# A planner that keeps the shared SBUF port of VectorE and GpSimd as a resource: decay attention and an expert layer on one core

## The chip, the core and the metric

The kernel runs on one core of a Trainium2 chip. TensorE (PE) multiplies matrices, VectorE (DVE), ScalarE (ACT) and GpSimd (POOL) work on elements, and SP issues most DMAs. The metric is the device time of one execution in microseconds; for several runs it is the median. The changed kernel will be compared with this one on the same chip.

## The reference

Attention with a decay per position (8 batches, 8 heads, 576 positions, 64 per head), and its output is the input of an expert layer (4608 tokens, 512 to 2048 to 512):

```python
scores = scale * np.matmul(q, k.transpose(0, 1, 3, 2))
log_f = np.log(np.clip(f, 0.0001, 1.0))
cum = np.cumsum(log_f, axis=-1)
decay = cum[:, :, :, None] - cum[:, :, None, :]
scores = np.where(causal, -1000000000.0, scores + decay)
scores = scores - np.max(scores, axis=-1, keepdims=True)
attn = np.exp(scores)
attn = attn / (np.sum(attn, axis=-1, keepdims=True) + 1e-09)
attn_out = np.matmul(attn, v)
...
h = x @ w_in
g = np.where(pos, h, np.where(neg, 0.0, (h + beta) ** 2 / (4.0 * beta)))
return g @ w_out
```

## The kernel before

**Two stages, run into each other.** Attention runs in 36 jobs: a job is a batch, a pair of heads and a range of row blocks of 128 positions (the first batch is cut in two ranges, so eight jobs). For each row block GpSimd makes the decay term (L965) and masks it (L969), TensorE makes the scores (L798 or L877), VectorE adds the two and takes the extreme of each row (L1002), ScalarE takes the exponential and its sum (L1011), a small addition on `nm` (L1017, on GpSimd or VectorE) and a reciprocal (L1023, VectorE) make the factor of each row. In the first eight jobs a diagonal matrix with these factors is made (`pr <- ident, nm`, on GpSimd, VectorE or ScalarE), TensorE transposes with it in float32 (L1052, L1058), and multiplies with v (L917). In later jobs the probabilities are split in a high and a low float16 part (L402 or L406, then L1087 on VectorE), a DMA transposes them and TensorE multiplies them (L927).

The expert layer runs in 18 chunks of 256 tokens by 8 blocks of 256 of the inner dimension: TensorE multiplies with w_in (L1150, tile `ph`), ScalarE and VectorE make `u` (L1159, L1162, L1163) and the two float16 parts of `g` (L402, L1169), TensorE multiplies with w_out (L1177, tile `po`).

**Weights.** Each of the 8 blocks of weights has two halves (w_in, w_out). `weight_split` rounds them in place on VectorE (L565, L569, L573, 128x1024 each), ScalarE takes the sum of absolute values (L577), a scale is found through a small transpose on TensorE (`across`, L450 to L465, whose two small steps `top` and `dg` run on VectorE or GpSimd), ScalarE writes the high float16 part (L593), and the low part is made either by VectorE in one instruction (L599) or by GpSimd in two (L601, L602). The raw weights lie in tiles `place` and `x` that are not yet in use, the results in `place`. `moe_scales` makes the scales `z` of the expert layer on GpSimd (L698) and VectorE; `join_scales` (L1121 to L1123) brings two batches to one scale.

**What sets the order.** No order is written out. Every piece of work is given to `Order.op` with its engine, a duration, what it reads and writes, and a priority; some pieces name other engines that may take them (`other`). `Order.plan` then plays through time with these durations: whenever an engine is free, the first piece by priority whose inputs are done and whose buffers can be had is taken, and a piece with several engines goes to the one that is free for it first. The result is one order of emission, and so the order of each engine's queue, the engine of each piece with a choice, and the buffers. On the chip each engine works off its queue in that order and waits only for semaphores; the plan's times play no part there. `OVER`, `AFTER` and the functions `act_us`, `dve_us`, `pool_us` hold the durations. Before, the durations of GpSimd's pieces were longer than they are when it runs alone, and nothing in the plan linked the two engines.

Of the kernel before, what the change touches and what calls it, by code (L numbers as in the profile page):

```python
# [72 lines left out]
class Order:  # L73
    AFTER = {"PE": 0.23, "DVE": 0.04, "ACT": 0.04, "POOL": 0.1, "DMA": 0.06}
    OVER = {"PE": 0.0, "DVE": 0.08, "ACT": 0.093, "POOL": -0.04}
# [9 lines left out]
    def op(self, eng, dur, emit, reads=(), writes=(), prio=0.0, size=0.0, mode=0, other=()):  # L85
        i = len(self.ops)
# [26 lines left out]
        self.ops.append([eng, dur, emit, deps, bufs, prio, size, mode, self.hold])  # L113
        return i

    def plan(self):
# [25 lines left out]
        while done < n:
# [5 lines left out]
            while again:  # L148
                again = False
                for eng, l in waiting.items():  # L150
# [111 lines left out]
def pool_us(n):  # L262
    return 0.3 + 0.00095 * n
# [11 lines left out]
def kernel(  # L275
# [115 lines left out]
    def V(n, emit, reads=(), writes=(), prio=0.0, us=None):  # L391
        op("DVE", us if us else dve_us(n), emit, reads, writes, prio)
# [4 lines left out]
    def G(us, emit, reads=(), writes=(), prio=0.0):  # L397
        op("POOL", us, emit, reads, writes, prio)
# [46 lines left out]
    def across(m, n, mkeys, prio):  # L445
# [17 lines left out]
        op("POOL", 0.7, make, ["ident"], [top, dg], prio, other=[("DVE", 0.4, 0.0)])  # L463
# [21 lines left out]
    def decay_sums():  # L485
# [71 lines left out]
    def weight_split(i, prio):  # L557
        ms = tiny("ms", 2, 2)
        for j in range(2):
# [8 lines left out]
            ), key, [bits], prio, 0.75)  # L568
# [3 lines left out]
            ), key, [bits], prio)  # L572
# [3 lines left out]
            ), [bits], key, prio)  # L576
# [10 lines left out]
        for j in range(2):  # L587
# [16 lines left out]
            op("POOL", 4.35, low, [("sw", i)], key + [("pl", i, j)], prio, other=[("DVE", 1.46, 0.0)])  # L604
# [66 lines left out]
    def moe_scales(b, k, first, last, prio):  # L671
# [38 lines left out]
        G(1.8, make, [("sv", b), ("rv", b), ("lim", k)] + need, [z.key], prio)  # L710
# [5 lines left out]
    def attention(ji):  # L716
# [11 lines left out]
        for j, src in enumerate((q, k)):  # L728
# [73 lines left out]
        else:  # L802
# [58 lines left out]
            V(640, klo, x32[1][2] + [sc, (qs, 1)], [(qs, 2)], pq)  # L861
            V(640, qlo, x32[0][2] + [sc, (qs, 0)], [(qs, 3)], pq)
# [19 lines left out]
        if p >= NPE:  # L882
# [14 lines left out]
            V(640, vlo, vkeys(hp) + [("sv", b), (vs, 0)], [(vs, 1)], pr - 2)  # L897
# [52 lines left out]
        for r in range(r0, r1):  # L950
# [5 lines left out]
            for h in range(2):  # L956
# [17 lines left out]
                G(1.08 + 0.0006 * wid if r < LAST else 1.25, decay, [cks[h], "sdz"] + sigkey, [(sd, h if r == LAST else 0)], pw)  # L974
# [296 lines left out]
```

## Time and profile before

| | us |
|---|---|
| median of 3 runs | 1097.66 (1097.19 to 1098.76) |
| the profiled execution | 1097.19 |
| its span | 1095.4 |
| TensorE busy | 1043.9 |
| VectorE busy | 804.9 |
| ScalarE busy | 729.3 |
| GpSimd busy | 575.2 |

In a row of a timeline stand the start, the length, the engine, the line, the operation, the tiles written and read, their shapes, the count, and in brackets how long the engine had been idle ahead of it and what ended that. In a row of stretches stand the stretch, its length, and for each engine the busy time and the number of instructions, then TensorE's granted clock as a share of full speed, the DMA engines' share and GB/s. In a row of one line's instructions stand the count, then the shortest, the median and the longest duration in ns. In a row of groups stand the count, the busy time in us, the mean in ns, and the idle time ahead of them.

### The profile page before, as it was taken

How to read it: one execution, taken by the hardware profiler on the slowest of the kernel's cores; microseconds unless marked ns; L12 is line 12 of the kernel's file. 1: busy time of each engine (PE TensorE's matmuls, PEld its weight loads, DVE VectorE, ACT ScalarE, POOL GpSimd, SP SyncE). 2: the span in 40 equal slices, each digit the busy share in tenths (PEclk: the TensorE clock that was granted, in tenths of full speed). 3: DMA queues.
4: the chain of work that ended last, by engine and by line, in shares of the span. 5: the costliest groups of instructions: out<-in, count | busy, mean ns of one | idle time of the engine just before them, and what ended most of it. 6: DMA issues, size and time to landing. Idle time of an engine off the chain costs nothing. (4 is left out here: it accounts for less than half of the span.)

```text
span 1095.4 us, 24735 instructions
## 1 busy us (share of the span) xinstructions
PE 1043.9 (95%) x8821; PEld 699.1 (64%) x8821; DVE 804.9 (73%) x2037; ACT 729.3 (67%) x1532; POOL 575.2 (53%) x1023
## 2 busy tenths in 40 slices
PE   6779898999999999999999999999999999999998
PEld 4445555556766666666766666666666777677665
DVE  6889888888778888878888878988887873232232
ACT  4666665767777777777777777777777874344343
POOL 4588866666666665557667656655666740000000
PEclk9889889999999999999999999999999999999999
DMA  7855446668788889778988788888778742000000
GB/s 199 267 153 146 145 105 122 134 107 188 140 176 157 159 163 187 140 153 155 172 167 167 154 166 158 169 168 158 146 147 173 124 105 51 1 20 21 1 20 20
DMA packets 389467, 145.32 MB, mean 133 GB/s; under 512 B 367200, under 2 KB 367200, under 8 KB 389344
## 3 DMA queue, kind: packets, MB, share of 16 engines
q1 hardware_dynamic: 383328, 132.21, 60.9%
q10 hardware_dynamic: 6016, 11.54, 3.0%
q8 instruction: 69, 1.13, 0.4%
q14 instruction: 54, 0.44, 0.1%
HBM read 64.63 MB, written 9.58 MB: 68 GB/s over the span
## 5 line engine op out<-in xcount | busy, mean ns | idle before, releaser
L1150 PE MATMUL ph<-x,place 128*128 128x256 f16 (+3 forms) x4608 | 409.6, 248 | 2.5 <-POOL place L602 1.2
L1177 PE MATMUL po<-place,g 128*128 128x512 f16 x1728 | 403.1, 381 | 1.0 <-ACT g L402 0.8
L1150 PEld LDWEIGHTS <-place 128*128 128x128 f16 x4608 | 357.0, 98 | 54.4 <-issue 5.1
L1177 PEld LDWEIGHTS <-g 128*128 128x128 f16 x1728 | 164.0, 98 | 185.9 <-issue 6.6
L1163 DVE SCALAR_TENSOR_TENSOR u<-ph,z,u 128x512 f32<-128x512 f32 x144 | 107.7, 749 | 127.0 <-ACT u L1162 126.2
L965 POOL TENSOR_SCALAR sdr<-ck,sg,cqs 128x128 f32<-128x128 f32 (+1 forms) x192 | 155.8, 812 | 68.2 <-DVE pr L1087 59.1
L1159 ACT ACTIVATE u<-ph,z 128x512 f32<-128x512 f32 x144 | 110.6, 768 | 103.6 <-PE ph L1150 98.5
L1011 ACT ACTIVATE sdr<-sdr,nm 128x512 f32<-128x512 f32 (+3 forms) x246 | 135.4, 551 | 52.5 <-DVE nm L1002 42.9
L1169 DVE SCALAR_TENSOR_TENSOR g<-u,z,g 128x512 f16<-128x512 f32 x144 | 112.0, 779 | 44.9 <-ACT g L402 44.3
L402 ACT ACTIVATE g<-u,z 128x512 f16<-128x512 f32 x141 | 101.2, 718 | 58.4 <-DVE u L1163 56.6
L1087 DVE SCALAR_TENSOR_TENSOR pr<-sdr,nm,pr 128x128 f16<-128x128 f32 (+1 forms) x224 | 122.3, 575 | 8.6 <-ACT pr L402 5.9
L969 POOL TENSOR_SCALAR_AFFINE_SELECT sdr<-sdr 128x128 f32<-128x128 f32 x246 | 100.6, 409 | 18.1
L1002 DVE CUSTOM_DVE_ANT_0 sdr<-s,sdr,sg 128x128 f32<-128x128 f32 (+1 forms) x192 | 100.6, 541 | 11.6 <-PE s L877 10.0
L402 ACT ACTIVATE pr<-sdr,nm 128x256 f16<-128x256 f32 (+3 forms) x151 | 78.1, 544 | 37.1 <-ACT sdr L1011 11.8
L877 PE MATMUL s<-qkT 128*128 128x128 f16 (+5 forms) x576 | 93.9, 298 | 4.0 <-DVE nm L1002 3.1
L1162 ACT ACTIVATE u<-u 128x512 f32<-128x512 f32 x144 | 90.5, 629 | 4.4
L927 PE MATMUL s<-pT,vs 128*64 128x320 f16 (+4 forms) x1176 | 70.1, 265 | 1.0 <-DVE x L944 0.8
L927 PEld LDWEIGHTS <-vs 128*64 128x64 f16 x1176 | 57.0, 110 | 21.2 <-issue 13.5
L877 PEld LDWEIGHTS <-qkT 128*128 128x128 f16 (+1 forms) x576 | 41.6, 101 | 33.4 <-issue 15.0
L1017 POOL TENSOR_SCALAR nm<-nm 128x2 f32<-128x2 f32 (+1 forms) x68 | 17.5, 257 | 82.7 <-ACT sdr L1011 75.8
L406 POOL TENSOR_SCALAR pr<-sdr,nm 128x512 f16<-128x512 f32 (+3 forms) x73 | 44.2, 608 | 28.5 <-DVE nm L1023 23.0
L965 POOL TENSOR_SCALAR sd<-ck,sg,cqs 64x576 f32<-64x576 f32 x48 | 42.2, 879 | 30.0 <-DVE pr L1087 27.1
(152 smaller groups left out, 1212.8 us busy)
## 6 DMA issues: line engine op xcount, KB each, us to landing
ck<-cum_d SPq DMA_DIRECT2D x62, 288.0 KB, 3.9
out_dram<-ot ACTq DMA_DIRECT2D x36, 256.0 KB, 3.6
v<-in_v_dram SPq DMA_DIRECT2D x64, 128.0 KB, 2.9
qk<-in_k_dram SPq DMA_DIRECT2D x64, 128.0 KB, 2.8
qkT<-qkT SPq DMA_DIRECT2D x48, 160.0 KB, 3.2
qk<-in_q_dram SPq DMA_DIRECT2D x56, 128.0 KB, 3.2
place<-in_moe_w_in_dram SPq DMA_DIRECT2D x8, 512.0 KB, 5.1
x<-in_moe_w_out_dram SPq DMA_DIRECT2D x8, 512.0 KB, 4.1
```

Source lines behind the costliest of these rows:

```text
L402: nc.scalar.activation(out, in_, AF.Copy, scale=scale)
L877: nc.tensor.matmul(sp[p0:p1, 0:c1 - c0], lhsT=tq[:, h, q0 - s0:q0 - s0 + p1 - p0], rhs=tk[:, h, c0:c1], start=(c == 0), stop=(c == 1),)
L927: nc.tensor.matmul(av.ap[64 * h:64 * h + 64, c0:n], lhsT=vs.ap[:, vl, h, t, :], rhs=pT.ap[:, t, pl, h, c0:n], start=(t == 0 and pi == 0), ...
L965: nc.gpsimd.tensor_scalar(out=sd.ap[p0:p1, 0:wid], in0=cks[h].ap[p0:p1, 0:wid], scalar1=ns if p < NQK else ns[p0:p1], scalar2=cqs()[p0:p1, ...
L969: nc.gpsimd.affine_select(sd.ap[p0:p1, q0:wid], sd.ap[p0:p1, q0:wid], pattern=[[-1, wid - q0]], channel_multiplier=1, base=0, compare_op=A ...
L1011: A(wid, lambda i=i, sd=sd, wid=wid, nm=nm, sm=sm: nc.scalar.activation(sd.ap[:, 0:wid], sd.ap[:, 0:wid], AF.Exp, bias=nm.ap[:, i:i + 1], ...
L1087: V(cols, lambda i=i, prv=prv, rows_=rows_, rc=rc: nc.vector.scalar_tensor_tensor(out=prv()[:, :, 1, i, :], in0=rows_(), scalar=rc.ap[:, i ...
L1150: nc.tensor.matmul(ph.ap[:, fi * TC + a0:fi * TC + a1], lhsT=wi[fb][:, wl, t, fi * P:(fi + 1) * P], rhs=xs[b][:, t, xl, s0:s0 + a1 - a0], ...
L1159: A(512, lambda i=i, ph=ph, u=u: nc.scalar.activation(u.ap, ph.ap, AF.Relu, scale=z.u[:, i:i + 1], bias=z.h[:, i:i + 1]), [ph, z.key], [u] ...
L1163: V(512, lambda i=i, ph=ph, u=u: nc.vector.scalar_tensor_tensor(out=u.ap, in0=ph.ap, scalar=z.t[:, i:i + 1], in1=u.ap, op0=ALU.max, op1=AL ...
L1169: V(512, lambda i=i, u=u, g=g: nc.vector.scalar_tensor_tensor(out=g.ap[:, 1], in0=u.ap, scalar=z.r[:, i:i + 1], in1=g.ap[:, 0], op0=ALU.mu ...
L1177: nc.tensor.matmul(po.ap[i], lhsT=g.ap[:, gl, fi * TC + i * P:fi * TC + (i + 1) * P], rhs=wo[fb][:, wl, fi, :], start=(fb == first and fi ...
```

## The change

`plan` gets one more time, `port`: until when the SBUF port that VectorE and GpSimd share is taken. A piece says through `port` on which engines it uses it. Nearly all of GpSimd's pieces do (not the memsets); on VectorE those do that read two operands from SBUF (the weight rows L565, L569, L573, the low parts L599, L849, L855, L892, L1087, L1169) and some small ones. A piece that uses the port isn't taken while the port is held for more than `PATIENCE` = 0.3 us longer; if less, it begins when the port comes free, and its engine is held from then. The durations of GpSimd's pieces, and of the weight rows on VectorE, are lowered. The low part of weights names VectorE first and GpSimd as the other, with 1.3 and 3.33 us in place of 1.46 and 4.35. No instruction is added or removed as such; the emission order, the engine of pieces with a choice, and the buffers follow from the new plan. Line numbers from L82 on grow by one to nine: L599 is now L608, L601 L610, L602 L611, L573 L582, L1017 L1026, L1163 L1172.

```diff
+PATIENCE = 0.3
...
+    RELEASE = {"DVE": 0.2, "POOL": 0.15}
...
+        port = 0.0
...
+                        if eng in ops[i][9] and port > t + PATIENCE:
+                            continue
...
+                        if eng in shared:
+                            begin = max(t, port)
+                            port = begin + dur - self.RELEASE[eng]
+                            heapq.heappush(events, max(t, port - PATIENCE))
...
 def pool_us(n):
-    return 0.3 + 0.00095 * n
+    return 0.26 + 0.00083 * n
...
-        op("POOL", 0.7, make, ["ident"], [top, dg], prio, other=[("DVE", 0.4, 0.0)])
+        op("POOL", 0.55, make, ["ident"], [top, dg], prio, other=[("DVE", 0.36, 0.0)], port=("POOL", "DVE") if n > 1 else ("POOL",))
...
-            ), key, [bits], prio, 0.75)
+            ), key, [bits], prio, 0.7, "DVE")
...
-            ), key, [bits], prio)
+            ), key, [bits], prio, 1.25, "DVE")
...
-            op("POOL", 4.35, low, [("sw", i)], key + [("pl", i, j)], prio, other=[("DVE", 1.46, 0.0)])
+            op("DVE", 1.3, low, [("sw", i)], key + [("pl", i, j)], prio, other=[("POOL", 3.33, 0.0)], port=("POOL", "DVE"))
...
-        G(1.8, make, [("sv", b), ("rv", b), ("lim", k)] + need, [z.key], prio)
+        G(1.25, make, [("sv", b), ("rv", b), ("lim", k)] + need, [z.key], prio)
...
-                G(1.08 + 0.0006 * wid if r < LAST else 1.25, decay, [cks[h], "sdz"] + sigkey, [(sd, h if r == LAST else 0)], pw)
+                G(0.6 + 0.00084 * wid if r < LAST else 1.03, decay, [cks[h], "sdz"] + sigkey, [(sd, h if r == LAST else 0)], pw)
...
-            op("POOL", 0.31, inverse, [(sm, i) for i in range(nh)], [rc], pw, other=[("DVE", 0.22, 0.0)])
+            op("POOL", 0.23, inverse, [(sm, i) for i in range(nh)], [rc], pw, other=[("DVE", 0.19, 0.0)], port=("POOL", "DVE") if nh > 1 else ("POOL",))
```

Every queue is in a new order from its first microseconds on. GpSimd has 1103 instructions in place of 1025, VectorE 1994 in place of 2039, ScalarE 1189 in place of 1222; TensorE and SP have as many as before. What moved to GpSimd: 32 of the additions on `nm`, 14 small steps of `across`, 14 scalings of q or k (`qs <- qk, sc`), 8 high parts of the last row block (`pr <- sd, nm`), and a few others. Of the 16 low parts of weights each of the two engines has eight, before and now, though not the same ones. The twelfth of the rows L1163 on VectorE stood behind 474 rows and stands behind 416. Three places:

The first is VectorE's queue around the first low part of weight block 0 (`place_82`); `nm` are the extremes and factors of rows, `s` the scores in PSUM, `ph` a PSUM tile. Before:

```order
L599 SCALAR_TENSOR_TENSOR place_82<-place_88,sw,place_82 128x1024
L1017 TENSOR_SCALAR nm_129<-nm_128 128x2
L1023 RECIPROCAL nm_129<-nm_129 128x2
L1002 ISA sdr_98,nm_130<-s_66,sdr_98 128x256
L1002 ISA nm_130 128x1
L404 TENSOR_SCALAR pr_101<-ident,nm_129 128x128
```

Now:

```order
L608 SCALAR_TENSOR_TENSOR place_82<-place_87,sw,place_82 128x1024
L953 SCALAR_TENSOR_TENSOR x_80<-s_67,sv,x_80 128x256
L421 COPY pT_0_109<-ph_69 128x4x128
L1011 ISA sdr_98,nm_129<-s_65,sdr_98 128x128
L1011 ISA nm_129 128x1
L1011 ISA sdr_99,nm_129<-s_66,sdr_99 128x128
L1011 ISA nm_129 128x1
L421 COPY qkT_108<-ph_70 128x256
L574 TENSOR_SCALAR qs<-place_89 128x1024
```

The addition behind the low part has gone to GpSimd, and rows that read PSUM stand there.

The second is GpSimd's queue at the same low part. Before, behind its own half of block 0:

```order
L965 TENSOR_SCALAR sdr_99<-pr_103,cq_78 128x256
L969 AFFINE_SELECT sdr_99<-sdr_99 128x128
L601 TENSOR_SCALAR place_87<-place_87,sw 128x1024
L602 TENSOR_TENSOR place_82<-place_87,place_82 128x1024
L1017 TENSOR_SCALAR nm_132<-nm_131 128x2
L406 TENSOR_SCALAR pr_102<-ident,nm_132 128x128
```

Now:

```order
L610 TENSOR_SCALAR place_88<-place_88,sw 128x1024
L611 TENSOR_TENSOR place_82<-place_88,place_82 128x1024
L1026 TENSOR_SCALAR nm_131<-nm_130 128x2
L974 TENSOR_SCALAR sdr_96<-ck_115,cq_78 128x128
L978 AFFINE_SELECT sdr_96<-sdr_96 128x128
L974 TENSOR_SCALAR sdr_97<-pr_103,cq_78 128x128
L978 AFFINE_SELECT sdr_97<-sdr_97 128x128
L1026 TENSOR_SCALAR nm_126<-nm_125 128x2
```

The low part has moved ahead of decay rows and of the additions of earlier row blocks (nm_131 is an addition of a row block that was done ahead of it before).

The third is where VectorE and GpSimd share later blocks. Before, VectorE around its low part of block 6 (`place_88`):

```order
L599 SCALAR_TENSOR_TENSOR place_88<-place_89,sw,place_88 128x1024
L565 TENSOR_SCALAR qs<-x_81 128x1024
L569 SCALAR_TENSOR_TENSOR qs<-x_81,qs 128x1024
L573 SCALAR_TENSOR_TENSOR x_81<-x_81,qs 128x1024
L1087 SCALAR_TENSOR_TENSOR pr_101<-sdr_98,nm_131,pr_101 128x128
```

Now VectorE around its low part of block 5 (`place_87`), and GpSimd at both low parts of block 6:

```order
L421 COPY qkT_108<-ph_69 128x192
L608 SCALAR_TENSOR_TENSOR place_87<-place_88,sw,place_87 128x1024
L582 SCALAR_TENSOR_TENSOR x_79<-x_79,qs 128x1024
L1096 SCALAR_TENSOR_TENSOR pr_101<-sdr_99,nm_131,pr_101 128x128
L1032 RECIPROCAL nm_126<-nm_126 128x2
L1011 ISA sdr_98,nm_127<-s_66,sdr_98 128x384
```

```order
L610 TENSOR_SCALAR place_89<-place_89,sw 128x1024
L611 TENSOR_TENSOR place_88<-place_89,place_88 128x1024
L610 TENSOR_SCALAR x_79<-x_79,sw 128x1024
L611 TENSOR_TENSOR place_88<-x_79,place_88 128x1024
L1026 TENSOR_SCALAR nm_125<-nm_132 128x2
L974 TENSOR_SCALAR sdr_98<-ck_115,cq_78 128x128
```

VectorE's split of the next weights no longer follows its low part in one run, three rows on SBUF operands still stand together, and GpSimd has two low parts one after the other, as it also has for a half of block 3 and a half of block 4. The product of the two scales in `join_scales` (L1122, now L1131) has no `port`.

More of the change, by code (lines that the diff above doesn't have):

```diff
@@ L83, with op @@
     hold = 0.0
-    def op(self, eng, dur, emit, reads=(), writes=(), prio=0.0, size=0.0, mode=0, other=()):
+    def op(self, eng, dur, emit, reads=(), writes=(), prio=0.0, size=0.0, mode=0, other=(), port=""):
         i = len(self.ops)
@@ L112, in op @@
                 b.pool.named += 1
-        self.ops.append([eng, dur, emit, deps, bufs, prio, size, mode, self.hold])
+        self.ops.append([eng, dur, emit, deps, bufs, prio, size, mode, self.hold, port])
         return i
@@ L389, with V, G @@
     lim = sb([P, 2, len(GROUPS) + 1], F32, "lim")
-    def V(n, emit, reads=(), writes=(), prio=0.0, us=None):
-        op("DVE", us if us else dve_us(n), emit, reads, writes, prio)
+    def V(n, emit, reads=(), writes=(), prio=0.0, us=None, port=""):
+        op("DVE", us if us else dve_us(n), emit, reads, writes, prio, port=port)
     def A(n, emit, reads=(), writes=(), prio=0.0, ptr=0, acc=0):
         op("ACT", act_us(n, ptr, acc), emit, reads, writes, prio)
-    def G(us, emit, reads=(), writes=(), prio=0.0):
-        op("POOL", us, emit, reads, writes, prio)
+    def G(us, emit, reads=(), writes=(), prio=0.0, port="POOL"):
+        op("POOL", us, emit, reads, writes, prio, port=port)
     def times(eng, out, in_, scale):
@@ L412, in copy, with X @@
             nc.vector.tensor_copy(out, in_)
-    def X(n, emit, reads=(), writes=(), prio=0.0, engs="AG", ptr=1, late=0.0):
+    def X(n, emit, reads=(), writes=(), prio=0.0, engs="AG", ptr=1, late=0.0, port=("POOL",)):
         us = {"A": ("ACT", act_us(n, ptr)), "D": ("DVE", dve_us(n)), "G": ("POOL", pool_us(n))}
         (first, t), *rest = [us[c] for c in engs]
-        op(first, t, emit, reads, writes, prio, other=[(e, u, late) for e, u in rest])
+        op(first, t, emit, reads, writes, prio, other=[(e, u, late) for e, u in rest], port=port)
     def M(us, emit, reads=(), writes=(), prio=0.0, mode=0):
@@ L575, in weight_split @@
                 op0=ALU.bitwise_and, op1=ALU.bitwise_or
-            ), [bits], key, prio)
+            ), [bits], key, prio, 1.25, "DVE")
             A(1024, lambda top=top, low=low, j=j: nc.scalar.activation(
@@ L860, in attention @@
             X(640, qhi, x32[0][2] + [sc], [(qs, 0), (qs, 5), (qs, 6)], pq)
-            V(640, klo, x32[1][2] + [sc, (qs, 1)], [(qs, 2)], pq)
-            V(640, qlo, x32[0][2] + [sc, (qs, 0)], [(qs, 3)], pq)
+            V(640, klo, x32[1][2] + [sc, (qs, 1)], [(qs, 2)], pq, port="DVE")
+            V(640, qlo, x32[0][2] + [sc, (qs, 0)], [(qs, 3)], pq, port="DVE")
             qt = Buf(qkt_pool)
@@ L895, in vlo @@
                 )
-            V(640, vlo, vkeys(hp) + [("sv", b), (vs, 0)], [(vs, 1)], pr - 2)
+            V(640, vlo, vkeys(hp) + [("sv", b), (vs, 0)], [(vs, 1)], pr - 2, port="DVE")
         pts = {}
@@ L1034, in attention @@
                         e, diag.ap[:, i * P:(i + 1) * P], ident, rc.ap[:, i:i + 1]
-                    ), [rc], [(diag, i)], pw + 0.5, "GDA")
+                    ), [rc], [(diag, i)], pw + 0.5, "GDA", port=("POOL", "DVE"))
                 n = P if r < LAST else 64
@@ L1089, in attention @@
                         op0=ALU.mult, op1=ALU.subtract,
-                    ), kk + [rc, (prb, i)], [(prb, 2 + i)], pw + 0.5)
+                    ), kk + [rc, (prb, i)], [(prb, 2 + i)], pw + 0.5, port="DVE")
                 def dst(pT=pT, r=r, o0=o0):
@@ L1170, in moe @@
                 out=g.ap[:, 1], in0=u.ap, scalar=z.r[:, i:i + 1], in1=g.ap[:, 0], op0=ALU.mult, op1=ALU.subtract
-            ), [u, z.key, (g, 0)], [(g, 1)], pf - 1e4)
+            ), [u, z.key, (g, 0)], [(g, 1)], pf - 1e4, port="DVE")
             def back(gl, fb=fb, g=g):
```

16 lines of the change are left out of this document (8 added, 8 removed).

## The prediction

> **What bounds the kernel.** I read the page first, then busy time by stage, then TensorE's idle time in order of time.
>
> ```profile
> span 1095.4 us, 24735 instructions
> PE 1043.9 (95%) x8821; PEld 699.1 (64%) x8821; DVE 804.9 (73%) x2037; ACT 729.3 (67%) x1532; POOL 575.2 (53%) x1023
> ...
> core 0: us, PE busy (x) PEld busy (x) DVE busy (x) ACT busy (x) POOL busy (x), PEclk, DMA share, GB/s
> 0.00:240.00 240.00, 200.50 (x1220) 125.34 (x1222) 200.38 (x510) 150.60 (x330) 159.69 (x260) 0.91 0.61 155
> 240.00:880.00 640.00, 633.01 (x5786) 428.72 (x5785) 528.73 (x1404) 483.61 (x1054) 406.28 (x747) 1.00 0.84 160
> 880.00:1095.40 215.40, 210.41 (x1819) 145.09 (x1817) 75.83 (x124) 95.06 (x151) 9.26 (x17) 1.00 0.11 26
> ```
>
> TensorE is the bound, and its work is the same in both kernels. What can change is its idle time, 51.5 us, and the time at a lower granted clock. From 240 to 880 us it idles 7.0 us, and after 880 us, where attention is over, 5.0 us. The first 240 us hold 39.5 us of idle time and a mean clock of 0.91. So the change is decided there. The first 8.5 us (the load of f and the scan) have nothing to reorder. The timeline of TensorE alone shows the rest; these eight rows are the later pauses over 1.3 us, with the one of 1.21 us (in brackets the idle time ahead of the row, and what ended it):
>
> ```profile
> 45.10 1.23 PE L1052 MATMUL ph<-pr,sdr 128*128 128x128 f32 x4 [3.65 <-ACT pr L402]
> 49.49 2.07 PE L1052 MATMUL ph<-pr,sdr 128*128 128x128 f32 x8 [2.44 <-POOL pr L406]
> 62.89 2.58 PE L1150 MATMUL ph<-x,place 128*128 128x256 f16 x22 [1.21 <-POOL place L602]
> 73.35 0.48 PE L798 MATMUL s<-qkT 64*64 64x64 f32 x4 [3.33 <-DVE nm L1002]
> 132.71 0.58 PE L465 MATMUL ph<-dg,ones 2*128 2x2 f32 x2 [2.53 <-POOL dg L459]
> 156.79 0.77 PE L787 MATMUL ph<-ident,qk 128*128 128x128 f32 x2 [2.69 <-DVE qkT L412]
> 186.19 0.53 PE L787 MATMUL ph<-ident,qk 128*128 128x128 f32 x2 [3.30 <-DVE rv L438]
> 214.05 0.53 PE L787 MATMUL ph<-ident,qk 128*128 128x128 f32 x2 [1.38 <-DVE u L1163]
> ```
>
> They sum to 20.5 us. Around such pauses the granted clock falls to half, in seven stretches; here are the first, the fourth, the last and the sum of all seven:
>
> ```profile
> 44.10:54.30 10.20, 6.75 (x29) 4.98 (x29) 9.47 (x19) 6.06 (x14) 2.45 (x5) 0.51 1.02 309
> 132.80:139.70 6.90, 6.90 (x33) 5.00 (x34) 6.27 (x8) 2.94 (x4) 6.39 (x8) 0.52 0.40 90
> 214.70:218.20 3.50, 3.49 (x15) 2.11 (x15) 3.46 (x10) 1.92 (x6) 1.37 (x5) 0.53 0.88 221
> sum 41.20, PE 35.70 PEld 22.51 DVE 34.98 ACT 26.68 POOL 24.96; mean PE 5.10 PEld 3.22 DVE 5.00 ACT 3.81 POOL 3.57
> ```
>
> TensorE was busy 35.7 us in them; at full clock that work takes half, so they cost up to 17.9 us. Pauses and clock together, 38.4 us, are the most that better timing can give in this stage.
>
> **Why those pauses.** Around the first one the timeline reads:
>
> ```profile
> 40.04 1.22 POOL L601 TENSOR_SCALAR place<-place,sw 128x1024 f32<-128x1024 f32 x1 [0.58 <-ACT place L593]
> 41.07 1.28 DVE L599 SCALAR_TENSOR_TENSOR place<-place,sw,place 128x1024 f16<-128x1024 f32 x1 [0.54 <-ACT place L593]
> 41.34 2.99 POOL L602 TENSOR_TENSOR place<-place,place 128x1024 f16<-128x1024 f32 x1
> 42.27 2.08 DVE L1017 TENSOR_SCALAR nm<-nm 128x2 f32<-128x2 f32 x1
> 44.39 0.17 DVE L1023 RECIPROCAL nm<-nm 128x2 f32<-128x2 f32 x1
> 44.65 0.40 ACT L402 ACTIVATE pr<-ident,nm 128x128 f32<-128x128 f32 x1 [2.49 <-DVE nm L1023]
> ...
> L1017 DVE TENSOR_SCALAR nm<-nm x92: 140/169/2083, 20.7 to 894.8; 128x2 f32<-128x2 f32 x69, 128x1 f32<-128x1 f32 x23
> ```
>
> An instruction on 128x2 numbers took 2.08 us, twelve times its median of 0.169, and ended with GpSimd's L602. Behind it waited the reciprocal, ScalarE's diagonal and TensorE. So VectorE and GpSimd lock each other out here, for whole instructions. At 156 us they do it in turns:
>
> ```profile
> 150.35 2.05 DVE L569 SCALAR_TENSOR_TENSOR qs<-x,qs 128x1024 int32<-128x1024 int32 x1
> 151.40 2.98 POOL L602 TENSOR_TENSOR place<-x,place 128x1024 f16<-128x1024 f32 x1
> 152.43 3.03 DVE L573 SCALAR_TENSOR_TENSOR x<-x,qs 128x1024 int32<-128x1024 int32 x1
> ...
> L573 DVE SCALAR_TENSOR_TENSOR place<-place,qs x9: 1204/1216/1994, 11.3 to 129.9; 128x1024 int32<-128x1024 int32 x9
> L602 POOL TENSOR_TENSOR place<-x,place x5: 2122/2981/2989, 79.5 to 181.7; 128x1024 f16<-128x1024 f32 x5
> ```
>
> L573 took 3.03 us instead of 1.22, and the copy queued behind it held TensorE for 2.69 us. The pause at 132.71 is the same from the other side: GpSimd's scale steps waited behind VectorE.
>
> ```profile
> 128.71 1.18 POOL L969 TENSOR_SCALAR_AFFINE_SELECT sdr<-sdr 128x128 f32<-128x128 f32 x1
> 129.88 1.32 POOL L698 TENSOR_SCALAR z<-sw,sv 128x3 f32<-128x3 f32 x1
> ...
> L969 POOL TENSOR_SCALAR_AFFINE_SELECT sdr<-sdr x246: 292/293/1182, 13.9 to 894.8; 128x128 f32<-128x128 f32 x123
> ```
>
> The Trainium skill says the same in "SBUF — State Buffer", section "Who interferes with whom": a VectorE instruction with two SBUF inputs, or in a mode that uses both ports, and a GpSimd instruction that reads SBUF exclude each other for the whole instruction, and issue order decides who blocks. The trace agrees (2.08 against 0.169). That rule also speaks against the change: a plan fixes each engine's own order, not which of two engines issues first. By it alone the sum is that of the first rival.
>
> **The change, part by part.** The number of instructions that TensorE and the DMA queues issue is the same. The only TensorE pause put down to a DMA after the start is 0.4 us, so SP's new order is taken at nothing; if a load came late, its pause would show with "DMA" as releaser.
>
> ```profile
> PE s L877 <- DMA qkT<-qkT: 0.4, 1, 0.4
> ```
>
> (a) First place, 41 to 54 us. Before, the addition L1017 stands right behind VectorE's low part. Now that addition is on GpSimd, and behind the low part on VectorE stand seven rows that read PSUM or finish such a row (copies, L1011, L953) before L574, the next that uses the port. So the lockout of 2.08 us goes, and with it I count the pause of 3.65 whole, half of the 2.44 behind it (its diagonal is still made on GpSimd behind VectorE's weight rows), and the stretch at half clock, 6.75/2 = 3.4: together 8.3 us.
>
> (b) The other six pauses, 14.4 us, and the other six stretches, (35.70-6.75)/2 = 14.5 us: 28.9 us, of which anything from none to all may go. At the second place shown, three users of the port (L608, L582, L1096) stand in a row on VectorE while GpSimd has its own low part, so collisions can go on. The join's product on VectorE isn't marked as a user of the port at all, and it cost 2 us behind the last low part:
>
> ```profile
> 181.75 2.12 DVE L1122 TENSOR_TENSOR join<-join,sv 128x1 f32<-128x1 f32 x1
> ```
>
> On the other side the expert layer comes sooner: the twelfth of its L1163 rows on VectorE stood behind 474 rows and stands behind 416, so TensorE has other work earlier. I take a quarter, 7.2 us, the end near "none", because of the two places just named.
>
> (c) What the change adds. GpSimd gets 78 instructions more. With the rows
>
> ```profile
> L1017 POOL TENSOR_SCALAR nm<-nm 128x2 f32<-128x2 f32 x59 | 14.4, 245 | 79.1 <-ACT sdr L1011 75.8 <-ACT pr L1011 1.8
> L406 POOL TENSOR_SCALAR qs<-qk,sc 128x640 f16<-128x640 f32 x7 | 6.9, 979 | 0.1
> L406 POOL TENSOR_SCALAR pr<-sd,nm 128x640 f16<-128x640 f32 x1 | 0.8, 793 | 0.1
> ```
>
> 14 scalings of q and k cost 13.7 us, 8 of the last row block 6.3, 23 additions 5.6. Nearly all lie in 240 to 880 us, where GpSimd is busy 406 of 640 us and TensorE, with expert work in hand, idles 7.0: I take them at nothing. Bounds from that row: 7.0 gained, or as much lost again. Early, though, GpSimd's queue has new waits. The addition nm_131 stands behind the low part of block 0 (L610 and L611: 1.22+2.12 us free, 4.2 as measured), and behind it four rows of decay sums; VectorE's reciprocal, the diagonal and TensorE's transposes wait for it. Twice, two low parts now stand back to back on GpSimd, 6.7 us free. Such a wait costs nothing where TensorE has other work in its order, and where it hasn't, about what the one at 132.71 cost: 2.53 + 6.90/2 = 6.0 us. There are three such places, so 0 to 18 us; I take one, 6.0.
>
> "VectorE first" for the low parts costs and gives nothing by itself: both engines stay candidates at once, and of 16 low parts each engine has eight, before and now.
>
> **Sum.** 8.3 + 7.2 - 6.0 = 9.5 us gained. The profiled execution took 1097.19 us (its span 1095.4 and 1.8 around it), so 1087.7; the median of the three runs shown is 0.5 above that execution: 1088.2.
>
> **Rivals.** *The collisions come back elsewhere* (or the plan doesn't do what it says on the chip). For it: order alone can't hold an engine back, and VectorE and GpSimd are busy 200 and 160 of the first 240 us, so someone meets someone. Against it: the first place is cleared by type of instruction, not by timing. Then (a) and (b) are offset by new lockouts of the same kind: 1097.7, give or take 3.
> *GpSimd's queue is late* and the change is slower. Place: the three waits of (c), in the first 200 us. Price 6.0 us each. It decides from three pauses on, since 15.5/6.0 = 2.6: with three 1097.7+2.5 = 1100.2, with four, one of them met twice, 1106. Against it: the additions that GpSimd had before took 0.245 us in the mean, and of its eight low parts TensorE was put down as waiting for one only, 1.21 us.
> *Most of it goes*: all of (a), 9.5, and half of (b), 14.5, with no new wait: 1073.7; all of it, 1059.3. The lockouts in the rows above speak for it, the two uncleared places against.
>
> **Chances.** Forecast (4 to 20 us gained) 0.58; collisions come back 0.18; GpSimd late 0.17; most of it goes 0.07. The range must leave out at most 2 in 10: from 1074, which leaves out the last case, to 1103, between three and four new pauses. A measurement of this kernel can tell about 0.2%, 2.2 us, from no change. Faster by more: 0.58 + 0.07 + 0.06 of the first rival = 0.71. Within: 0.10, most of it from the first rival. Slower: 0.04 + 0.15 = 0.19.
>
> **What would show it.** (a): no VectorE addition of 2 us between 35 and 60 us, no TensorE pause over 3 us there, the first half-clock stretch shorter than 10.2 us. (b): the longest times of L582 and L608 near their medians, less than 41.2 us at half clock. (c): TensorE pauses that end on GpSimd's nm, dg or z rows. 240 to 880 us: idle time near 7 us. I am wrong if the summed pauses of the first 240 us are as long as before, or if idle time appears after 240 us, where I count none.

## The result, and the profile after

| | before | after |
|---|---|---|
| median, us | 1097.53 (1097.19 to 1098.76, 4 runs) | 1085.97 (1081.36 to 1087.77, 4 runs) |
| profiled execution, us | 1097.19 | 1081.36 |
| its span, us | 1095.4 | 1079.6 |

The ratio, worked out over all runs and not from the two medians, is 0.9886 (95%: 0.9852 to 0.9921). By the medians after is 11.6 us faster, where 9.5 were forecast. The profiled execution of after is the fastest of its four, so its span is 15.8 us shorter, and the parts below add up to that figure and not to 11.6.

The head of after's page, then its busy time by stage (columns as in the prediction):

```profile
span 1079.6 us, 24790 instructions
PE 1038.0 (96%) x8821; PEld 696.3 (64%) x8821; DVE 793.6 (74%) x1992; ACT 708.0 (66%) x1499; POOL 613.7 (57%) x1101
```

```profile
0.00:240.00 240.00, 211.00 (x1325) 133.73 (x1327) 200.80 (x511) 156.81 (x344) 167.40 (x285) 0.94 0.62 159
240.00:880.00 640.00, 632.38 (x5868) 428.84 (x5865) 530.49 (x1395) 469.22 (x1036) 445.30 (x816) 1.00 0.86 161
880.00:1079.60 199.60, 194.57 (x1634) 133.74 (x1631) 62.31 (x89) 82.00 (x120) 0.99 (x2) 1.00 0.08 20
```

TensorE's idle time in the first 240 us fell from 39.5 to 29.0 us. From 240 to 880 us it is 7.6 (before 7.0), after 880 us 5.0 as before. TensorE is also busy 5.9 us less for the same 8821 instructions, mostly since it runs less at half clock (4.5 of the 5.9, by the stretches below). So the gain is made in the first 240 us and collected at the end, where the last stretch is 15.8 us shorter.

Where in that stage? The same view of TensorE alone, in two stretches, first of before, then of after (behind the busy time the granted clock, DMA share, GB/s):

```profile
33.00:60.00 27.00, 18.38 (x116) 0.81 0.70 207
60.00:240.00 180.00, 159.40 (x1020) 0.91 0.57 133
```

```profile
33.00:60.00 27.00, 20.70 (x98) 0.62 0.62 199
60.00:240.00 180.00, 167.86 (x1137) 0.97 0.59 139
```

Between 33 and 60 us TensorE idles 2.3 us less, but its clock is lower, and it issues 98 matmuls where it issued 116: that stretch got worse. After 60 us idle time falls from 20.6 to 12.1 us and the clock rises from 0.91 to 0.97: there lies the gain. The stretches at half clock in after are three in place of seven:

```profile
38.50:59.10 20.60, 16.48 (x73) 11.41 (x71) 14.11 (x38) 10.97 (x25) 11.30 (x14) 0.52 0.55 159
120.40:127.30 6.90, 6.75 (x32) 5.07 (x33) 4.05 (x11) 1.48 (x5) 3.93 (x9) 0.55 1.00 321
140.90:144.40 3.50, 3.50 (x12) 1.25 (x10) 3.50 (x10) 3.19 (x7) 2.41 (x2) 0.60 0.72 163
sum 31.00, PE 26.73 PEld 17.73 DVE 21.67 ACT 15.65 POOL 17.64; mean PE 8.91 PEld 5.91 DVE 7.22 ACT 5.22 POOL 5.88
```

Half of the busy time in them is the loss, as in the prediction: 26.73/2 = 13.4 us, before 17.9. (These three windows lie up to 0.7 us late: in finer ones the first stretch runs from 37.8 to 58.3 us, and the loss of all three is 12.9.) The first stretch doubled from 10.2 to 20.6 us.

TensorE's timeline in after, all pauses over 1.3 us behind the start:

```profile
21.36 1.07 PE L807 MATMUL s<-qkT 64*128 64x128 f32 x4 [1.73 <-ACT qkT L419]
36.97 0.89 PE L807 MATMUL s<-qkT 64*128 64x128 f32 x4 [2.07 <-DVE x L953]
47.65 0.37 PE L459 MATMUL ph<-ident,ms 128*2 128x128 f32 x1 [1.78 <-ACT x L586]
63.74 0.27 PE L459 MATMUL ph<-ident,ms 128*2 128x128 f32 x1 [1.37 <-ACT qkT L419]
120.55 1.41 PE L796 MATMUL ph<-ident,qk 128*128 128x128 f32 x5 [3.81 <-DVE pT L421]
171.06 0.48 PE L807 MATMUL s<-qkT 64*128 64x128 f32 x2 [1.63 <-DVE nm L1011]
```

Only two are over 2 us, and these two are lockouts again. Ahead of the first, a weight row on VectorE (L574) met GpSimd's low part; ahead of the second, three small instructions of VectorE (128x3 and 128x1 numbers) met two low parts back to back on GpSimd (timelines of after):

```profile
33.85 2.12 POOL L611 TENSOR_TENSOR place<-place,place 128x1024 f16<-128x1024 f32 x1
33.96 2.56 DVE L574 TENSOR_SCALAR qs<-place 128x1024 int32<-128x1024 int32 x1
...
114.39 2.15 POOL L611 TENSOR_TENSOR place<-place,place 128x1024 f16<-128x1024 f32 x1
114.45 2.12 DVE L450 TENSOR_SCALAR rw<-rw 128x3 int32<-128x3 int32 x1
116.69 1.01 DVE L671 TENSOR_TENSOR rw<-mp 128x3 f32<-128x3 f32 x1
117.77 2.11 POOL L611 TENSOR_TENSOR place<-place,place 128x1024 f16<-128x1024 f32 x1
117.87 2.03 DVE L1016 TENSOR_TENSOR nm<-nm 128x1 f32<-128x1 f32 x1
```

L671 ended with L610, the first half of the second low part (116.52 us, 1.17 long). Behind L1016 stood the copy `pT` that TensorE waited 3.81 us for. L574 reads one operand from SBUF, not two as the description of the change has it for all weight rows, and is locked out all the same. L450 and L671 are not marked as users of the port in the plan; L574 and L1016 are, and met GpSimd all the same, since the plan fixes an order and not a time.

What did go is most of the lockouts of the low parts of weights. By line (count: shortest, median, longest in ns), first two forms of before that the prediction has no row for, then after:

```profile
L602 POOL TENSOR_TENSOR place<-place,place x3: 2960/2986/3006, 41.3 to 98.2; 128x1024 f16<-128x1024 f32 x3
L599 DVE SCALAR_TENSOR_TENSOR place<-place,sw,place x6: 1279/1339/2398, 41.1 to 148.3; 128x1024 f16<-128x1024 f32 x6
```

```profile
L611 POOL TENSOR_TENSOR place<-x,place x3: 2132/2306/3026, 143.2 to 192.4; 128x1024 f16<-128x1024 f32 x3
L611 POOL TENSOR_TENSOR place<-place,place x5: 2112/2127/2149, 33.8 to 163.4; 128x1024 f16<-128x1024 f32 x5
L608 DVE SCALAR_TENSOR_TENSOR place<-place,sw,place x4: 1285/1296/1315, 31.0 to 142.9; 128x1024 f16<-128x1024 f32 x4
L608 DVE SCALAR_TENSOR_TENSOR place<-x,sw,place x4: 1267/1303/1419, 59.6 to 194.3; 128x1024 f16<-128x1024 f32 x4
L582 DVE SCALAR_TENSOR_TENSOR x<-x,qs x7: 1203/1226/3148, 45.1 to 179.3; 128x1024 int32<-128x1024 int32 x7
L1026 DVE TENSOR_SCALAR nm<-nm x60: 138/169/750, 68.8 to 877.8; 128x2 f32<-128x2 f32 x46, 128x1 f32<-128x1 f32 x14
```

GpSimd's half of the low part from `x` had a median of 2.98 us and has 2.31 (of three, one still 3.03), the one from `place` had 2.99 and has 2.13, with none over 2.15; on VectorE the longest was 2.40, and is 1.42. VectorE's longest addition on `nm` fell from 2.08 to 0.75. The weight row L582 still has one of 3.15, at 144 us.

### The profile page after: what moved, and what is told of

Its sections match the earlier page's. It is cut to its first block, busy times and chain, and to the rows that moved or that the text cites. A ratio compares the mean times of both kernels' runs of the same rounds, so it can differ in the third digit from the quotient of the medians.

```text
span 1079.6 us, 24790 instructions
## 1 busy us (share of the span) xinstructions
PE 1038.0 (96%) x8821; PEld 696.3 (64%) x8821; DVE 793.6 (74%) x1992; ACT 708.0 (66%) x1499; POOL 613.7 (57%) x1101
## 5 line engine op out<-in xcount | busy, mean ns | idle before, releaser
L1172 DVE SCALAR_TENSOR_TENSOR u<-ph,z,u 128x512 f32<-128x512 f32 x144 | 107.7, 748 | 125.8 <-ACT u L1171 124.7
L1178 DVE SCALAR_TENSOR_TENSOR g<-u,z,g 128x512 f16<-128x512 f32 x144 | 114.8, 797 | 42.5 <-ACT g L411 41.0
L411 ACT ACTIVATE g<-u,z 128x512 f16<-128x512 f32 x138 | 99.0, 717 | 53.9 <-DVE u L1172 52.5
L1011 DVE CUSTOM_DVE_ANT_0 sdr<-s,sdr,sg 128x128 f32<-128x128 f32 (+1 forms) x192 | 101.5, 542 | 21.9 <-PE s L886 10.9
L978 POOL TENSOR_SCALAR_AFFINE_SELECT sdr<-sdr 128x128 f32<-128x128 f32 x246 | 104.3, 424 | 18.1
L411 ACT ACTIVATE pr<-sdr,nm 128x128 f16<-128x128 f32 (+3 forms) x145 | 75.7, 546 | 44.0 <-issue 17.5
L886 PE MATMUL s<-qkT 128*128 128x128 f16 (+5 forms) x576 | 90.1, 298 | 2.0 <-DVE nm L1011 1.0
L1026 POOL TENSOR_SCALAR nm<-nm 128x2 f32<-128x2 f32 (+1 forms) x100 | 32.2, 322 | 67.0 <-ACT sdr L1020 47.0
L936 PE MATMUL s<-pT,vs 128*64 128x320 f16 (+4 forms) x1176 | 67.7, 263 | 2.5 <-DVE x L953 0.8
L886 PEld LDWEIGHTS <-qkT 128*128 128x128 f16 (+1 forms) x576 | 40.2, 101 | 30.7 <-issue 14.8
L415 POOL TENSOR_SCALAR pr<-sdr,nm 128x384 f16<-128x384 f32 (+3 forms) x79 | 48.5, 616 | 19.9 <-DVE nm L1032 16.8
```

What stands on the lines that cost most here:

```text
L411: nc.scalar.activation(out, in_, AF.Copy, scale=scale)
L886: nc.tensor.matmul(sp[p0:p1, 0:c1 - c0], lhsT=tq[:, h, q0 - s0:q0 - s0 + p1 - p0], rhs=tk[:, h, c0:c1], start=(c == 0), stop=(c == 1),)
L936: nc.tensor.matmul(av.ap[64 * h:64 * h + 64, c0:n], lhsT=vs.ap[:, vl, h, t, :], rhs=pT.ap[:, t, pl, h, c0:n], start=(t == 0 and pi == 0), ...
L978: nc.gpsimd.affine_select(sd.ap[p0:p1, q0:wid], sd.ap[p0:p1, q0:wid], pattern=[[-1, wid - q0]], channel_multiplier=1, base=0, compare_op=A ...
L1172: V(512, lambda i=i, ph=ph, u=u: nc.vector.scalar_tensor_tensor(out=u.ap, in0=ph.ap, scalar=z.t[:, i:i + 1], in1=u.ap, op0=ALU.max, op1=AL ...
L1178: V(512, lambda i=i, u=u, g=g: nc.vector.scalar_tensor_tensor(out=g.ap[:, 1], in0=u.ap, scalar=z.r[:, i:i + 1], in1=g.ap[:, 0], op0=ALU.mu ...
```

## The experiments

The kernel before ran beside each of them on the same chip; its medians there are 1097.31 to 1097.40 us. Ratios are against it.

**The two halves of the change.** Does the rule gain, or do the durations? First the rule with the old durations:

```diff
-    return 0.26 + 0.00083 * n
+    return 0.3 + 0.00095 * n
...
-            op("DVE", 1.3, low, [("sw", i)], key + [("pl", i, j)], prio, other=[("POOL", 3.33, 0.0)], port=("POOL", "DVE"))
+            op("POOL", 4.35, low, [("sw", i)], key + [("pl", i, j)], prio, other=[("DVE", 1.46, 0.0)], port=("POOL", "DVE"))
```

and so for every duration that the change lowers.

> The changed kernel with its port rule, and all durations as they were before the change (GpSimd's long ones, the weight rows, the low parts with GpSimd first at 4.35 and VectorE at 1.46). Three theories. Collisions: it is the port rule that keeps lockouts off TensorE's path, so most of the gain stays, 1082 to 1092 us, and no TensorE pause over 3 us in 20 to 220 us. Durations: the lower durations give the gain (another share of work on GpSimd), so 1095 to 1100. Scatter: any other plan moves the time by some 10 us either way, and the result says nothing of the rule: anything from 1085 to 1110.

Measured: 1096.79 us (1095.30 to 1097.91, 10 runs), ratio 0.9996 (0.9986 to 1.0005). No gain, though on the chip the low parts are the cleanest of all kernels (by line, rule alone):

```profile
L611 POOL TENSOR_TENSOR place<-x,place x4: 2125/2138/2162, 95.8 to 193.2; 128x1024 f16<-128x1024 f32 x4
L608 DVE SCALAR_TENSOR_TENSOR place<-place,sw,place x5: 1275/1285/1452, 60.3 to 158.6; 128x1024 f16<-128x1024 f32 x5
```

So fewer lockouts are not by themselves a shorter time. TensorE's longest pause in this kernel is 5.52 us, at 143 us, longer than any of before behind the start. It ends a wait for GpSimd's rows that make the scales `z` (L707): they stand behind GpSimd's low part in its own queue, and then the first takes 1.24 us beside VectorE's weight rows, where the median is 0.27. So a pause can come from the order in one queue as well, and lockouts other than those of the low parts were left. Its stages show what was lost:

```profile
0.00:240.00 240.00, 206.03 (x1270) 131.13 (x1272) 180.10 (x470) 154.56 (x333) 145.00 (x244) 0.91 0.58 151
240.00:880.00 640.00, 628.13 (x5722) 425.38 (x5719) 514.95 (x1382) 477.88 (x1051) 395.44 (x756) 0.99 0.85 159
```

Against before, TensorE idles 5.5 us less in the first stage (34.0 for 39.5) and 4.9 more in the second (11.9 for 7.0). GpSimd does 145.0 us of work in the first stage where after does 167.4, VectorE 180.1 where it does 200.8, and TensorE idles 11.9 us in the second stage (after 7.6). My reading, which these rows fit but don't prove: the old durations already held the time lost to the port, so with the rule it is counted twice, and the plan holds engines back that could work.

Then the durations without the rule:

```diff
-                        if eng in ops[i][9] and port > t + PATIENCE:
-                            continue
...
-                        if eng in shared:
-                            begin = max(t, port)
-                            port = begin + dur - self.RELEASE[eng]
-                            heapq.heappush(events, max(t, port - PATIENCE))
```

> The changed kernel with its new durations, but the plan holds no port (the two places that use it are taken out). Collisions: the gain is gone, 1094 to 1102 us, and pauses over 2.4 us behind 2 us lockouts are back in the first 220 us. Durations: the gain stays, 1083 to 1090. Scatter: anything from 1085 to 1110.

Measured: 1127.85 us (1126.38 to 1130.24, 4 runs), ratio 1.0283 (1.0261 to 1.0305): 30 us slower than before, outside every range that was expected. Its two later stages, and then TensorE's longest sum of waits from 240 to 880 us (total, times, longest):

```profile
240.00:880.00 640.00, 611.79 (x5532) 410.71 (x5530) 516.63 (x1352) 450.44 (x981) 416.44 (x750) 1.00 0.81 155
880.00:1126.50 246.50, 239.83 (x2087) 163.99 (x2085) 96.68 (x178) 112.94 (x192) 27.12 (x51) 1.00 0.18 38
```

```profile
PE s L880 <- DVE nm L1005: 12.4, 22, 2.4
```

From 240 to 880 us TensorE idles 28.2 us, 12.4 of it for the extremes of rows on VectorE; in after, the same wait (there L886 on L1011) is 1.0. GpSimd works 27.1 us after 880, where in after it has 1.0: attention is late and the end is longer. I read it so: with short durations and no rule the plan is too hopeful about GpSimd and VectorE, and the rule lets the durations be short. So neither half brought the gain, and together they do. Each half was run with one plan only: the 30 us are more than any spread between plans shown below, but "no gain" of the rule alone is known no better than that spread, some 8 us.

**What the lockout of the additions costs.** Kernel before, its order kept; each addition of two columns on VectorE is issued as two of one column:

```diff
-                (nc.gpsimd if e == "POOL" else nc.vector).tensor_scalar(
-                    out=rc.ap[:, 0:nh], in0=sm.ap[:, 0:nh], scalar1=1e-9, ...
+                for a, z in ((0, nh),) if e == "POOL" else [(i, i + 1) for i in range(nh)]:
+                    (nc.gpsimd if e == "POOL" else nc.vector).tensor_scalar(
+                        out=rc.ap[:, a:z], in0=sm.ap[:, a:z], scalar1=1e-9, ...
```

> The kernel before, its order and engines kept, but each addition L1017 that runs on VectorE on 128x2 numbers is issued as two on 128x1. Collisions, with the price of the first place as the prediction has it: a one-column addition doesn't take the port, so the 2.08 us lockout at 42 us becomes two of about 0.15, the TensorE pause of 3.65 us ends below 1.8, the half-clock stretch behind it gets shorter, and the time falls by 2 to 7 us, to 1090 to 1096. Rival: the pause has another cause (GpSimd's low part itself, or ScalarE), or the one-column form is locked out as well: pause 3 us or more, 1096 to 1100.

Measured: 1092.39 us (1090.64 to 1096.49, 10 runs), ratio 0.9957 (0.9945 to 0.9969), which is 4.7 us for all 69 such additions. At the first place, VectorE's timeline and then TensorE's:

```profile
42.32 0.21 DVE L1018 TENSOR_SCALAR nm<-nm 128x1 f32<-128x1 f32 x2
...
43.03 1.43 DVE L404 TENSOR_SCALAR pr<-ident,nm 128x128 f32<-128x128 f32 x1
```

```profile
43.28 0.49 PE L1053 MATMUL ph<-pr,sdr 128*128 128x128 f32 x2 [1.80 <-ACT pr L402]
```

Two columns take 0.21 us where the one instruction took 2.08, and the pause of 3.65 becomes 1.80. But the next instruction that uses the port is locked out in its place: the diagonal L404 takes 1.43 us (median 0.29) until GpSimd's L602 ends at 44.38 us, and TensorE idles 0.75 us more for it. The next pause (2.44) becomes 2.78, and the first half-clock stretch stays 10.2 us. So the lockout is real and the edit pays, but it was half of that pause at most and none of the stretch. Nor are the 4.7 us the price of this one place: of the 4.6 us between the profiled spans 1.8 are idle time and 2.8 busy time, and no row ties them to this place.

**How much is one plan's luck?** A planner turns a hair's change into another order. Three jolts, each to the plan of before and to that of after: a constant of the model is moved by a few per cent, nothing else.

```diff
-    AFTER = {"PE": 0.23, "DVE": 0.04, "ACT": 0.04, "POOL": 0.1, "DMA": 0.06}
+    AFTER = {"PE": 0.24, "DVE": 0.04, "ACT": 0.04, "POOL": 0.1, "DMA": 0.06}
```

in the first pair, 0.22 in the second; in the third, ScalarE's fixed cost:

```diff
-    return 0.18 + 0.00084 * n + (0.1 if ptr else 0.0) + (0.05 if ptr > 1 else 0.0) + 0.19 * acc
+    return 0.185 + 0.00084 * n + (0.1 if ptr else 0.0) + (0.05 if ptr > 1 else 0.0) + 0.19 * acc
```

The first pair:

> The kernel before, with one constant of its plan moved by a hair (the time after a TensorE piece 0.24 in place of 0.23 us); from about VectorE's 62nd row on every queue is in another order, and no rule is new. Collisions and durations: no better a plan, so within 4 us of the kernel before, 1094 to 1102. Scatter: off by more than 5 us, either way.

> The changed kernel with the same jolt as e4 (0.24 in place of 0.23 us after a TensorE piece): rule and durations kept, another order from about VectorE's 84th row on. Rule: the new plan is better as a kind, so 1080 to 1092 again. Scatter: the 1086 of the changed kernel was one draw among plans that lie some 8 us to both sides of the old one, so a value of 1092 to 1105 is as likely as one below.

The second:

> The kernel before with the same opposite jolt (0.22 us), another order from VectorE's 176th row on. Rule, now that e4 gave 1089: plans of the old kind lie around 1090 to 1105, so this one too. Scatter: the same kind of values as the jolted changed kernels give, 1085 to 1105.

> The changed kernel with the opposite jolt (0.22 us after a TensorE piece), another order from VectorE's 5th row on. Rule: 1080 to 1092. Scatter: 1085 to 1105, with 1092 or more as likely as not.

The third, and after once more as it is:

> The kernel before with a third jolt (each ScalarE piece 5 ns longer in the plan), another order from VectorE's 141st row on. Rule: plans of the old kind have given 1097, 1089 and 1094; this one lies in 1088 to 1100, above every plan of the new kind so far (1081 to 1086). Scatter: as likely below 1086 as above.

> The changed kernel with the same third jolt, another order from VectorE's 84th row on. Rule: 1079 to 1088. Scatter: 1081 to 1100, above 1088 as likely as not.

> The changed kernel once more, on the chip and in the rounds of e9 to e11. All theories: 1081 to 1088, within 0.4% of its first time of 1086; it is there to be set beside e11 and the jolted ones.

| plan | without the change, us | with it, us | TensorE idle, 0 to 240 us |
|---|---|---|---|
| as it is | 1097.53 | 1085.97; again 1081.90 (1080.41 to 1087.12) | 39.5; 29.0, again 30.3 |
| 0.24 | 1089.33 (1088.47 to 1090.88) | 1080.78 (1077.60 to 1085.86) | 35.5; 26.3 |
| 0.22 | 1094.11 (1091.58 to 1096.37) | 1082.20 (1080.70 to 1085.43) | 37.6; 30.5 |
| 0.185 | 1095.30 (1092.64 to 1097.73) | 1081.15 (1078.81 to 1083.24) | 37.1; 28.1 |

The ratios of the three jolts of before are 0.9932 (0.9917 to 0.9947), 0.9967 (0.9951 to 0.9984) and 0.9976 (0.9964 to 0.9987): each is faster than before by more than its interval, without any rule for the port. So the kernel before is the worst of its four, and the four medians lie 8.2 us apart. The first of these jolts came out below the range that collisions and durations gave for it (1094 to 1102), and off by 8 us, as scatter would have it. Scatter alone would also have put some plans with the change above 1092, and none is there. With the change, the four plans lie between 1080.8 and 1086.0. The two groups of medians don't overlap: their means are 1094.1 and 1082.0 (the repeated plan taken once, at the mean of its two), 12 us apart. In each pair TensorE idles some 7 to 10 us less in the first 240 us. The gain belongs to the rule with its durations; of the size of one pair, some us are luck (the pairs give 8.6 to 14.2). Two rows of the stage from 0 to 240 us stand for the groups, the best of each (0.24), without and with the change:

```profile
0.00:240.00 240.00, 204.53 (x1298) 126.75 (x1299) 205.29 (x533) 160.17 (x352) 151.37 (x261) 0.94 0.63 159
```

```profile
0.00:240.00 240.00, 213.72 (x1313) 134.78 (x1314) 199.32 (x506) 156.29 (x341) 166.34 (x285) 0.96 0.61 158
```

**The lockouts that are left.** Kernel after, order kept: the small instructions that collided are issued in a form that didn't. The additions by columns as above, the steps of `weight_limits` by columns, and where two columns are multiplied or compared, the second goes in as a scalar per partition:

```diff
-                nc.vector.tensor_tensor(out=rw[:, 2, blocks], in0=mp[:, 0, blocks], in1=mp[:, 1, blocks], op=ALU.mult)
+                for c in range(first, last + 1):
+                    nc.vector.tensor_scalar(
+                        out=rw[:, 2, c:c + 1], in0=mp[:, 0, c:c + 1], scalar1=mp[:, 1, c:c + 1], scalar2=None, op0=ALU.mult
+                    )
...
-                    V(0, lambda nm=nm: nc.vector.tensor_tensor(
-                        out=nm.ap[:, 0:1], in0=nm.ap[:, 0:1], in1=nm.ap[:, 1:2], op=ALU.min
+                    V(0, lambda nm=nm: nc.vector.tensor_scalar(
+                        out=nm.ap[:, 0:1], in0=nm.ap[:, 0:1], scalar1=nm.ap[:, 1:2], scalar2=None, op0=ALU.min
```

> The changed kernel, its order and engines kept, but small VectorE instructions in a form that doesn't take the port: the additions L1026 and the integer steps of the weight limits by single columns, and three products or minima of two tiny SBUF operands as an operation with a pointer to the scalar. Collisions: the pause of 3.81 us at 120 us, behind three such instructions of 2.12, 1.01 and 2.03 us, falls below 1.5; the time falls by 2 to 6 us against the changed kernel, to 1080 to 1084. Rival: the small instructions only stood in the shadow of GpSimd's low parts, VectorE's next large one is locked out in their place, and the time stays within 2 us, 1084 to 1088; if a pointer operand also takes the port, the three still show 1 us or more.

Measured: 1081.38 us (1076.58 to 1084.67, 4 runs), ratio 0.9835 (0.9807 to 0.9864). The timeline of VectorE, with the GpSimd row that they met:

```profile
114.82 2.14 POOL L611 TENSOR_TENSOR place<-place,place 128x1024 f16<-128x1024 f32 x1
115.22 0.15 DVE L450 TENSOR_SCALAR rw<-rw 128x1 int32<-128x1 int32 x1
115.50 0.43 DVE L673 TENSOR_SCALAR rw<-mp 128x1 f32<-128x1 f32 x3
116.10 0.20 DVE L1020 TENSOR_SCALAR nm<-nm 128x1 f32<-128x1 f32 x1
...
118.89 2.53 DVE L608 SCALAR_TENSOR_TENSOR place<-x,sw,place 128x1024 f16<-128x1024 f32 x1
```

What took 2.12, 1.01 and 2.03 us in after (L450, L671, L1016) takes 0.15 for each of three columns, 0.43 and 0.20 here, while GpSimd's low part runs, and the pause of 3.81 is gone. A low part on VectorE takes 2.53 us in their place, but no pause of TensorE ends on it. So it is shown that the form took these lockouts and this pause away. A gain in time is not: TensorE idles 29.9 us in the first 240 us (after 29.0, again 30.3), since other pauses are longer (2.50 at 64 us in place of 1.37; 1.79 at 134 us, 1.75 at 196), and the runs overlap with those of after (1085.97, again 1081.90). The same edit on the best plan (0.24):

> The jolted changed kernel of e5 with the small VectorE instructions in the form without the port, as in e8. Collisions: its pause of 3.79 us at 122 us, the same as the changed kernel's, falls below 1.5, and the time falls by 2 to 5 us against e5, to 1076 to 1079, the fastest of all. Rival: within 2 us of e5, 1079 to 1083.

Measured: 1077.20 us (1075.33 to 1078.20, 4 runs), ratio 0.9812 (0.9799 to 0.9826), where that plan without the edit had 0.9849 (0.9816 to 0.9882). Its pause of 3.79 us at 122 us is gone as well:

```profile
122.13 1.41 PE L796 MATMUL ph<-ident,qk 128*128 128x128 f32 x5 [3.79 <-DVE pT L421]
```

is the row of the plan without the edit; with it, no pause from 100 to 130 us is over 0.8 us. This kernel has the lowest time of all, 20 us under before, and 9 and 5 under the two medians of after. Against its own plan without the edit it is 3.6 us, with intervals of the ratios that just overlap, and the first 240 us don't show the gain (idle time 27.2 us, without the edit 26.3, though there the slowest of four executions is the profiled one).

## Why the prediction came out, step by step

**The sum** was 9.5 us, and 11.6 were measured (15.8 in the profiled execution). But its terms were not right: two errors of opposite sign nearly cancel, so that the sum came so near is luck. By the stretches above, in the profiled executions:

- *(a), first place: forecast 8.3 gained; in truth the stretch from 33 to 60 us lost 2.5.* Idle time fell by 2.3 us (3.65 + 1.22 were counted), and at half clock 16.48/2 - 6.75/2 = 4.9 us more were lost, where 3.4 fewer were counted. The lockout of L1017 did go, as said, and no pause over 3 us is left there. What failed is the step "the lockout of 2.08 us goes, and with it I count the pause of 3.65 whole ... and the stretch at half clock". Taking the lockout away alone ended 1.85 us of that pause, of which 0.75 came back behind the next locked instruction, and nothing of the stretch; and the new order put another lockout, L574 behind L611, ahead of the same place.
- *(b), the rest: forecast a quarter of 28.9, 7.2 us; in truth about 25.* From 60 to 240 us idle time fell by 8.5 us although the place of (c) cost 3.81 in it, so 12.3 went elsewhere; the loss by half clock fell from 14.5 to (26.73 - 16.48)/2 = 5.1, with 3.4 of (c) in it, so 12.7. The sign was right and the size was not. The two places that I named as reasons to stay near "none" are locked out less than I thought: the join's product has 0.64 us at most, L582 still has its 3.15 at 144 us, but TensorE has no pause of 1 us between 140 and 169. The four plans without the change explain a part: the jolts alone took 2 to 8 us off the time, so some of these pauses were probably this plan's bad luck, which another order can lose without any rule. How much of the 25 is that, and how much the change, one pair can't tell; over four pairs the share of rule and durations in the whole is 12.
- *(c), the price: forecast one bad place in three at 6.0 us; one place, 3.81 + 6.75/2 = 7.2.* It is where two low parts stand back to back on GpSimd, as feared. But the wait ran through VectorE's small instructions, not through GpSimd's queue: TensorE's waits on GpSimd's rows are small (the largest sum of after: total, times, longest):

```profile
PE ph L474 <- POOL dg L468: 1.6, 3, 0.8
```

- *GpSimd's further work from 240 to 880 us at nothing*: it was busy 39 us more there (the prediction's rows came to 25.6, with 23 of the 32 additions counted), and TensorE idled 7.6 in place of 7.0. Right; but in the plan with the short durations and no rule TensorE idled 28.2 there.
- *"VectorE first" at nothing*: right. With the two names exchanged, each with its duration, the plan gives the same order on every engine, so no run is needed.
- *"38.4 us, the most that better timing can give"* counts only the pauses that it lists. All idle time of the first 240 us behind the start is 39.5 - 8.5 = 31.0 us, so with the clock the bound was 48.9. The forecast doesn't hang on it.

From the terms: -2.5 + 25.0 - 7.2 = 15.3; the 0.3 us that TensorE idled more before 33 us and the 0.6 more from 240 to 880 leave 14.4. The other 1.4 us of the 15.8 come as busy time, which fell by 5.9 where the clock accounts for 4.5; these rows don't show why.

**The rivals.** "The collisions come back elsewhere" happened, at 34 and 114 us, but cost less than went. "GpSimd's queue is late" did not. "Most of it goes" is what happened in (b), and would have been the outcome, had (a) and (c) not taken 9.7 us.

**The rule against the change** ("SBUF — State Buffer" of the Trainium skill, "Who interferes with whom": issue order decides who waits) is borne out by L574, which the plan had kept apart and the chip did not: 2.56 us against its median of 0.693. It doesn't give the time, since four plans of four gained.

**Open.** The nine runs of after lie 7.4 us apart (1080.41 to 1087.77), 45 of before beside the experiments 4.9 (1095.86 to 1100.77); why is not settled. Why a jolt of before gains 8 us or 2 isn't either, nor how much of the rule's 12 us is lockouts that went and how much the shorter durations' better order.

## What to carry to other kernels

When two engines share a lock, a planner may need both halves: the lock as a resource and durations free of contention. Here the lock with long durations gained nothing, perhaps because it is counted twice, and short durations without it lost 30 us. Judge a planner's rule by several plans, each moved by a hair, because one pair compares two lucky or unlucky orders (here 8 us between plans of the same kind). And where a small instruction waits for a large one's lock, look for a form of it that needs no lock: that changes no order, though the next instruction may be locked out in its place.

## What the runs showed of the hardware

**The form decides, and being small is no protection.** An addition on 128x2 numbers waits 2.08 us behind GpSimd, two on 128x1 take 0.21 together. A minimum of two 128x1 columns from SBUF takes 2.03 us; with the second one as a scalar per partition it takes 0.20. The Trainium skill ("SBUF — State Buffer", "Who interferes with whom") tells of VectorE instructions with two SBUF inputs, or in a mode that uses both ports, as those that exclude GpSimd; the rows agree for the minimum (2.03 us), and a scalar operand doesn't act as a second input (0.20).

**Half clock without a long pause.** Busy time of TensorE in after in steps of 3.4 us around its first stretch:

```profile
35.10:38.50 3.40, 1.53 (x7) 0.90 0.99 381
38.50:41.90 3.40, 3.40 (x14) 0.50 0.99 359
41.90:45.30 3.40, 2.71 (x14) 0.50 0.81 159
45.30:48.70 3.40, 0.94 (x4) 0.50 0.67 148
48.70:52.10 3.40, 2.43 (x10) 0.50 0.84 297
52.10:55.50 3.40, 3.40 (x19) 0.50 0.00 0
55.50:58.90 3.40, 3.40 (x19) 0.58 0.00 0
```

No pause here is over 2.1 us. Finer windows put the fall at 37.8 us and the return at 58.3. In the 3.4 us ahead of the fall TensorE was busy 1.33 us; the step behind it was full (37.8 to 41.2: 3.40), and the clock stayed at half. It came back behind two steps that were full or nearly so (3.16 of 3.5 us, 3.40 of 3.4). The Trainium skill ("TensorE: Matmul & The Clock Gate", "Part 1: The HAM clock gate") tells of half clock after an idle window of about 3.4 us and of its release after a busy one; here a window less than half busy was enough, and the full one behind the fall did not release it, while at 140 us one full step did (140.2 to 143.6: 3.40, then full clock). I read it so: the pauses of 0.7 to 1.8 us inside the stretch, each cheap by itself, kept the clock at half, and made the first place dearer though its largest lockout had gone. No run tried that alone.
